# Expert layers of a fused attention and mixture-of-experts kernel: the last float64 conversion step of each expert moved into its first layer, two softmax operations rewritten, and row transposes on full blocks

## The chip, the cores and the metric

The kernel runs on one core of one Trainium2 chip. The time is the device time of one execution in microseconds (us), first instruction to last with what lies around them. A core has TensorE for matrix products (PE in the rows, with PEld for the loading of its stationary operand), VectorE (DVE), ScalarE (ACT), GpSimd (POOL) and SyncE (SP), whose queue here only issues transfers. All of them run their own instructions in order and wait for one another through semaphores.

## The reference

Three parts follow each other: a recurrent attention over 768 steps, a mixture of 8 experts in which each of the 3072 rows goes to the expert with the largest logit, and a dense layer of width 2048.

```python
def _moe_ref(x, w_gate, w_output_gate, w1, w2):
    logits = x @ w_gate
    e_idx = np.argmax(logits, axis=1)
    probs = np.exp(logits - logits.max(-1, keepdims=True))
    probs /= probs.sum(-1, keepdims=True) + 1e-09
    gate_w = probs[np.arange(N), e_idx]
    eom = 1.0 / (1.0 + np.exp(-(x @ w_output_gate)))
    for e in range(E):
        mask = e_idx == e
        h = np.maximum(x[mask] @ w1[e], 0.0)
        out[mask] = gate_w[mask, None] * eom[mask, e, None] * (h @ w2[e])

def _moe2_ref(x, w_in, w_out):
    h = np.maximum(x @ w_in, 0.0)
    return (h * h @ w_out).astype(np.float32)
```

The weights w_in and w_out of the dense layer come as float64; all else is float32.

## The kernel before

The attention comes first; while it runs, the rows are sorted by expert in DRAM. Then the experts follow, in the order 0 to 7, written out by hand instruction by instruction (nothing reorders them), and then the dense layer.

**An expert.** Up to 448 rows of an expert stand transposed in `x3`. The *first layer* has eight parts f = 0 to 7: eight matmuls with 448 columns fill `ph` in PSUM (three buffers), and `hidden` empties it: ScalarE writes the rectified high part (L1304), VectorE the low part (L1305). A `ph` buffer is free again when VectorE is done with it, so part f + 3 of TensorE waits for VectorE's part f. At the ends of f = 5, 6 and 7, `trans_x` transposes a third of the next expert's rows each (L1277, four blocks of up to 128 rows; the last block has 64), which `split_x` splits on ScalarE and VectorE. The *second layer* has 64 matmuls (L1408) in eight groups t = 0 to 7; `beside(e, t, gate)` issues the work of other engines at the start of each group. Its three results `py` are copied by ScalarE (L1415, then L1413 twice) and stored. Expert 0 is split: its first 256 rows run through all f ahead of the loop over the experts, the other rows in the loop.

**Weight pieces.** `drain(later, 1)` converts one piece of the next expert's weights: ScalarE rounds it (L920), GpSimd subtracts (L921), and SP then issues the load of a later piece (L958). Four pieces are in f = 0 to 3, four at t = 0, 2, 4 and 6. After the last expert's pieces come those of w_in.

**Conversion steps.** `Narrow` turns w_in and w_out from float64 into float32, in 32 pieces. `narrow.load()` issues the load of a piece (q, L1185). `narrow.step()` number i issues the store of piece i - 2 from ScalarE's queue (L1206), converts piece i (ScalarE L1193, VectorE L1194 to L1197, GpSimd L1198), and finishes piece i - 1 on VectorE (L1211). 34 steps are needed. One stands at the end of expert 0's first 256 rows, four in each second layer at t = 1, 3, 5 and 7, and one behind the last expert.

**Factors.** `gates` computes the rows' factors for `gt` at t = 1 to 3: maximum and difference on VectorE (L1023, L1024), two exponentials on ScalarE (L1026, L1027), then on VectorE a copy (L1029), a sum (L1031), an addition (L1032), and three more small operations (L1033 to L1035).

**The dense layer** begins with `stage1`: eight matmuls with 512 columns into `ph2` (two buffers), emptied by ScalarE (L1454) and squared and split by VectorE and ScalarE (L1455 to L1457). `stage2` (L1229 to L1231) multiplies by w_out.

Of the kernel before, what the change touches and what calls it, by code (L numbers as in the profile page):

```python
# [12 lines left out]
AF = mybir.ActivationFunctionType  # L13
ALU = mybir.AluOpType
# [10 lines left out]
E = 8  # L25
# [798 lines left out]
def program(tc, A, out, nch=NCH, order=ORDER):  # L824
    nc = tc.nc
    V, G, S_, P = nc.vector, nc.gpsimd, nc.scalar, nc.tensor
    with ExitStack() as top:
# [113 lines left out]
        def drain(g, n=10**6):  # L941
            for _ in range(n):
                if next(g, "end") == "end":
                    return
# [71 lines left out]
        def gates(pool, x, g, e):  # L1016


            a8 = list(x.shape[:-1]) + [8]
            L, O = x[..., 0:8], x[..., 8 + e]  # L1020
            d = pool.tile(a8, F32, name="gd", bufs=1)
            m = pool.tile(a8[:-1], F32, name="gm", bufs=1)
            V.tensor_reduce(out=m, in_=L, axis=AX.X, op=ALU.max)  # L1023
            V.tensor_tensor(out=d, in0=L, in1=m.unsqueeze(len(a8) - 1).to_broadcast(a8), op=ALU.subtract)  # L1024
            yield
            S_.activation(d, d, AF.Exp)  # L1026
            S_.activation(g[..., 1], O, AF.Exp, scale=-1.0)  # L1027
            yield
            V.tensor_copy(g[..., 0], x[..., 16])  # L1029
            g = g[..., 1]  # L1030
            V.tensor_reduce(out=m, in_=d, axis=AX.X, op=ALU.add)  # L1031
            V.tensor_scalar(out=m, in0=m, scalar1=1e-9, scalar2=None, op0=ALU.add)  # L1032
            V.scalar_tensor_tensor(out=g, in0=g, scalar=1.0, in1=m, op0=ALU.add, op1=ALU.mult)  # L1033
            V.reciprocal(g, g)
            V.tensor_tensor(out=g, in0=g, in1=g, op=ALU.mult)  # L1035

# [235 lines left out]

        def transpose(t, pk, ks, js):
            for j in js:
                n = NBLK[j]
                for k in ks:
                    P.transpose(pk[k][:, 128 * j : 128 * j + n], t[0:n, j, 128 * k : 128 * k + 128], ident[0:n, 0:n])  # L1277

        with ExitStack() as ctx:
            ep = ctx.enter_context(tc.tile_pool(name="ep", bufs=1))  # L1280
# [32 lines left out]
            with tc.manual_schedule():  # L1313
                S_.activation(fl[:, 0:1], cst[0:1, 0:1], AF.Exp)
                load_x(0)
                trans_x(0, range(3), raws[:, 3].rearrange("p (j x)->p j x", j=2), range(2))
                py = psy.tile([128, 320], F32, name="py", tag="py")
                for _ in range(4):
                    P.matmul(py[:, 0:128], ident, ident, start=True, stop=True)
                drain(first_w[0])  # L1320
                cur = parts(ring[0], 6144)
                narrow = Narrow()
                later = stream([(e % 2, A["we"][e], W1E) for e in range(1, E)] + [(0, wiD, W2I)], before)
                drain(later, 1)
                load_x(1)
                h = [ep.tile([128, 2 * CAP], F32R, name="hw", bufs=9) for f in range(8)]
                for f in range(8):
                    ph = psh.tile([128, CAP], F32, name="ph")
                    first(ph[:, 0:256], *cur, F1, f, x3[0], slice(0, 256))
                    hidden(ph, h[f], slice(0, 256))  # L1330
                    if f == 5:
                        trans_x(0, range(3), None, range(2, 4))
                    if f in (4, 7):
                        drain(later, 1)
                    if f < 4:
                        narrow.load()
                    if f == 7:
                        narrow.step()

                def put(j, n, off, gt):  # L1340
                    why = "the experts have at most S * B rows together"
                    p = min(n, 128)
                    at = nc.s_assert_within(off + 128 * j, 0, YR - n, skip_runtime_bounds_check_because=why)
                    nc.sync.dma_start(out=gtD[bass.ds(at, n)].rearrange("(j p) x->p j x", p=p), in_=gt[0:p, j : j + n // p])

                def factors(e, off):

                    gt = mp.tile([128, 4, 2], F32, name="gt", bufs=2)
                    yield from gates(mp, glog.pop(e), gt, e)
                    yield  # L1350
                    put(0, 384, off, gt)
                    rest.append((3, 64, off, gt))

                def beside(e, t, gate):

                    if t == 0 and e + 2 < E:
                        load_x(e + 2)
                    if t % 2 == 0:
                        drain(later, 1)
                    else:  # L1360
                        narrow.step()
                    if t == 2:
                        narrow.load()
                    if t > 0:
                        drain(gate, 1)

                glog, rest = {}, []
                for e in range(E):
                    hi, lo = parts(ring[e % 2], 6144)
                    gl = glog[e] = mp.tile([128, 4, 18], F32, name="gl", bufs=2)  # L1370
                    S_.activation(gl, xg[e][:, :, 384:XW], AF.Copy)
                    if e == E - 1:
                        load_y(E)
                    off = nc.values_load(oi[0:1, e : e + 1], engines=[mybir.EngineType.SP], min_val=0, max_val=Y0 + S * B)
                    if e:
                        h = [ep.tile([128, 2 * CAP], F32R, name="hw", bufs=9) for f in range(8)]
                    for f in range(8):
                        ph = psh.tile([128, CAP], F32, name="ph")
                        c = slice(0 if e else 192, CAP)
                        first(ph[:, c], hi, lo, F1, f, x3[e], c)  # L1380
                        hidden(ph, h[f], slice(0 if e else 256, CAP))
                        if f in (range(4) if e else (1, 3)):
                            drain(later, 1)
                        if e and 4 <= f < 7:
                            narrow.load()
                        if f == 7 and rest:
                            put(*rest.pop())
                        if f >= 5:
                            if e + 1 < E:
                                trans_x(e + 1, [f - 5])  # L1390
                            else:
                                split_y(E, f - 5)
                    gate = factors(e, off)
                    why = "the experts have at most S * B rows together"
                    col = nc.s_assert_within(off, 0, YR - CAP, skip_runtime_bounds_check_because=why)
                    wc = ring[e % 2][:, 5120:6144].bitcast(F32R)

                    seq = [(2, f, k) for f in range(8) for k in range(2)] + [(m, f, k) for m in range(2) for f in range(8) for k in range(3)]
                    for i, (m, f, k) in enumerate(seq):
                        if i % 8 == 0:  # L1400
                            beside(e, i // 8, gate)
                        last = f == 7 and k == 2 - (m == 2)
                        if f == 0 and k == 0:
                            py = psy.tile([128, CAP], F32, name="py", tag="py")
                        x = h[f][:, CAP * (k == 1) : CAP * (k == 1) + CAP]
                        c = 3072 + 256 * f + 128 * m
                        w = (hi, hi, lo)[k][:, c : c + 128] if m < 2 else wc[:, 128 * f : 128 * f + 128]
                        P.matmul(py, w, x, start=(f == 0 and k == 0), stop=last)  # L1408
                        if last:
                            yT = xp.tile([128, CAP], F32, name="yT", bufs=3)  # L1410
                            n = 128 if m < 2 else 64
                            if m < 2:
                                S_.activation(yT, py, AF.Copy)  # L1413
                            else:
                                S_.activation(yT[0:64], py[64:128], AF.Copy)  # L1415
                                V.tensor_tensor(out=yT[0:64], in0=py[0:64], in1=yT[0:64], op=ALU.add)
                            nc.sync.dma_start(out=yTD[128 * m : 128 * m + n, bass.ds(col, CAP)], in_=yT[0:n])
                    drain(gate)
                narrow.step()
                assert narrow.at >= len(narrow.todo) + 2  # L1420


# [106 lines left out]
```

## Time and profile before

| | |
|---|---|
| median of 3 runs | 1053.68 us (1048.99 to 1054.67) |
| the profiled execution | 1044.5 us, of which the span from first to last instruction is 1042.7 us |
| attention | 0 to 442 us |
| experts | 442 to 681 us |
| dense layer | 681 to 1042.7 us |
| mean granted TensorE clock | 0.971 of full speed |

The profiled execution was 9.2 us shorter than the median of the runs. Times of a part are read from the trace, in us from the span's start. Durations of single instructions are in us, or in ns where a row says mean ns.

### The profile page before, as it was taken

How to read it: one execution, taken by the hardware profiler on the slowest of the kernel's cores; microseconds unless marked ns; L12 is line 12 of the kernel's file. 1: busy time of each engine (PE TensorE's matmuls, PEld its weight loads, DVE VectorE, ACT ScalarE, POOL GpSimd, SP SyncE). 2: the span in 40 equal slices, each digit the busy share in tenths (PEclk: the TensorE clock that was granted, in tenths of full speed). 3: DMA queues.
4: the chain of work that ended last, by engine and by line, in shares of the span. 5: the costliest groups of instructions: out<-in, count | busy, mean ns of one | idle time of the engine just before them, and what ended most of it. 6: DMA issues, size and time to landing. Idle time of an engine off the chain costs nothing.

```text
span 1042.7 us, 33206 instructions
## 1 busy us (share of the span) xinstructions
PE 945.3 (91%) x13882; PEld 832.5 (80%) x13882; DVE 689.9 (66%) x1768; ACT 606.8 (58%) x1350; POOL 464.0 (45%) x449
## 2 busy tenths in 40 slices
PE   1679988989898988799999999989999999999997
PEld 1567777877777776688888889979988899988986
DVE  5889999899888985447777777665444343434341
ACT  3568987978888888345554455544433343433332
POOL 5657777676777764337655666620010101010101
PEclk9789999999999998889999999999999999999999
DMA  3864444444434426286898787763101010000000
GB/s 107 262 183 127 126 133 120 116 114 107 127 105 128 123 58 171 65 268 162 227 240 229 231 224 191 228 121 73 42 13 31 26 31 26 1 26 1 14 13 26
DMA packets 59314, 120.33 MB, mean 115 GB/s; under 512 B 14608, under 2 KB 32144, under 8 KB 57232
## 3 DMA queue, kind: packets, MB, share of 16 engines
q1 hardware_dynamic: 51424, 103.09, 35.8%
q10 hardware_dynamic: 5040, 6.12, 2.6%
q0 software_dynamic: 2688, 8.88, 2.5%
q8 instruction: 112, 1.84, 0.8%
q14 instruction: 50, 0.41, 0.1%
HBM read 92.01 MB, written 26.05 MB: 113 GB/s over the span
## 4 chain that ended last, share of the span: by engine, by line
PE 66%; DVE 16%; ACT 7%; DMA 6%; issue 4%; SPq 1%; POOL 1%; POOLq 0%; ACTq 0%; DVEq 0%
PE ph L1226 24%; PE po L1230 5%; PE po L1229 5%; PE po L1231 5%; PE py L1408 4%; PE ST L659 3%; PE tp L696 2%; DMA q<-in_wi_dram 2%; ACT sT L676 2%; PE sc L715 2%; PE kt L543 2%; PE y L732 2%; PE R L629 2%; DVE c L1194 2%; PE lg L872 1%
## 5 line engine op out<-in xcount | busy, mean ns | idle before, releaser
L1226 PE MATMUL ph<-x,ring 128*128 128x512 f32 (+2 forms) x1344 | 311.8, 380 | 9.6 <-DVE hw L1305 5.8
L1226 PEld LDWEIGHTS ph<-x,ring 128*128 128x128 f32 x1344 | 241.7, 191 | 46.4 <-DVE hw L1305 8.1
L1480 POOL DMA_INDIRECT out_dram<-o,TID x24 | 27.8, 1158 | 322.7 <-ACT o L1478 281.4
L921 POOL TENSOR_TENSOR ring<-raws,ring 128x732 fp32r<-128x732 f32 (+2 forms) x72 | 123.7, 1734 | 59.4 <-DVE x L1220 28.0
L1455 DVE TENSOR_TENSOR q<-r 128x512 f32<-128x512 f32 x96 | 66.5, 692 | 121.9 <-ACT r L1454 121.9
L1454 ACT ACTIVATE r<-ph 128x512 f32<-128x512 f32 x96 | 57.3, 597 | 126.6 <-PE ph L1226 124.3
L486 POOL TENSOR_TENSOR arena<-arena 40x1024 f32<-40x1024 f32 x43 | 105.6, 2455 | 36.4 <-DVE arena L468 12.1
L1229 PE MATMUL po<-ring,hh 128*128 128x320 f32 x368 | 114.2, 310 | 0.0
L1230 PE MATMUL po<-ring,hl 128*128 128x320 f32 x368 | 114.1, 310 | 0.0
L1231 PE MATMUL po<-ring,hh 128*128 128x320 f32 x368 | 113.8, 309 | 0.0
L1457 DVE TENSOR_TENSOR hl<-q,hh 128x512 fp32r<-128x512 f32 x92 | 63.8, 693 | 64.2 <-ACT hh L1456 64.2
L1408 PE MATMUL py<-hw,ring 128*128 128x448 f32 x512 | 105.8, 367 | 0.0
L1408 PEld LDWEIGHTS py<-hw,ring 128*128 128x128 f32 x512 | 95.6, 188 | 7.9
L1456 ACT ACTIVATE hh<-q 128x512 fp32r<-128x512 f32 x92 | 58.1, 632 | 70.1 <-DVE q L1455 70.1
L1229 PEld LDWEIGHTS po<-ring,hh 128*128 128x128 f32 x368 | 69.6, 189 | 4.3
L1230 PEld LDWEIGHTS po<-ring,hl 128*128 128x128 f32 x368 | 69.4, 189 | 3.9
L1305 DVE SCALAR_TENSOR_TENSOR hw<-ph,hw 128x448 fp32r<-128x448 f32 (+2 forms) x72 | 40.0, 570 | 49.1 <-ACT hw L1304 49.0
L1231 PEld LDWEIGHTS po<-ring,hh 128*128 128x128 f32 x368 | 69.3, 188 | 0.0
L1304 ACT ACTIVATE hw<-ph 128x448 fp32r<-128x448 f32 (+2 forms) x72 | 36.0, 501 | 42.2 <-PE ph L1226 42.1
L1198 POOL TENSOR_TENSOR c<-c,r 128x384 int32<-128x384 int32 (+1 forms) x32 | 35.1, 1097 | 52.0 <-issue 15.6
L920 ACT ACTIVATE ring<-raws 128x732 fp32r<-128x732 f32 (+2 forms) x72 | 57.0, 794 | 1.5 <-DMA raws<-in_we_dram 1.1
L676 ACT ACTIVATE sT<-ST 40x320 f32<-40x320 f32 x88 | 33.1, 424 | 34.7 <-PE ST L659 34.5
(214 smaller groups left out, 1974.1 us busy)
## 6 DMA issues: line engine op xcount, KB each, us to landing
raws<-in_we_dram SPq DMA_DIRECT2D x48, 366.0 KB
arena<-in_xE_dram SPq DMA_DIRECT2D x48, 322.5 KB
xL<-in_xL_dram SPq DMA_DIRECT2D x24, 480.0 KB
xsD<-raws SPq DMA_DIRECT2D x24, 268.0 KB
q<-in_wi_dram SPq DMA_DIRECT2D x16, 384.0 KB
xg<-xsD SPq DMA_DIRECT2D x7, 804.0 KB
q<-in_wo_dram SPq DMA_DIRECT2D x16, 320.0 KB
wb<-in_wB_dram SPq DMA_DIRECT2D x24, 165.0 KB
```

The costliest lines, as they stand in the source:

```text
L486: (V if c < EARLY[2 + hh] else G).tensor_tensor(out=bd[sl, :, :, hh].rearrange("p a b c l j->p (a b) c (l j)"), in0=s["bk"][sl].rearrange( ...
L920: S_.activation(hi, rw, AF.Copy)
L921: G.tensor_tensor(out=lo, in0=rw, in1=hi.bitcast(F32), op=ALU.subtract)
L1226: P.matmul(ps, t[:, o : o + 128], x3[:, i, c], start=(j == 0), stop=(j == 7))
L1229: P.matmul(ps, hh, whi[:, o : o + 320], start=start, stop=False)
L1230: P.matmul(ps, hl, whi[:, o : o + 320], start=False, stop=False)
L1231: P.matmul(ps, hh, wlo[:, o : o + 320], start=False, stop=stop)
L1408: P.matmul(py, w, x, start=(f == 0 and k == 0), stop=last)
L1454: S_.activation(r, ph, AF.Relu)
L1455: V.tensor_tensor(out=q, in0=r, in1=r, op=ALU.mult)
L1456: S_.activation(hh, q, AF.Copy)
L1457: V.tensor_tensor(out=hl, in0=q, in1=hh.bitcast(F32), op=ALU.subtract)
```

## The change

Three edits stand side by side.

1. The steps of `Narrow` at t = 7 are gone, and so are the one at the end of expert 0's first 256 rows and the one behind the last expert. In their place, each expert has a step in the middle of its first layer, behind `hidden` of f = 4. Expert 7 has two more, at t = 6 and t = 7, which only finish and store the last pieces. There are still 34 steps in the same order.
2. In `gates`, the copy into `g[..., 0]` and the addition of 1 run on ScalarE, and the addition of 1e-9 is joined to the multiplication: four VectorE operations become two, and ScalarE gets two.
3. `transpose` takes 128 rows for the last block as well. Its rows 64 to 127 are computed and not used.

```diff
-            V.tensor_copy(g[..., 0], x[..., 16])
+            S_.activation(g[..., 0], x[..., 16], AF.Copy)
             g = g[..., 1]
+            S_.activation(g, g, AF.Copy, bias=1.0)
             V.tensor_reduce(out=m, in_=d, axis=AX.X, op=ALU.add)
-            V.tensor_scalar(out=m, in0=m, scalar1=1e-9, scalar2=None, op0=ALU.add)
-            V.scalar_tensor_tensor(out=g, in0=g, scalar=1.0, in1=m, op0=ALU.add, op1=ALU.mult)
+            V.scalar_tensor_tensor(out=g, in0=m, scalar=1e-9, in1=g, op0=ALU.add, op1=ALU.mult)
...
             for j in js:
-                n = NBLK[j]
                 for k in ks:
-                    P.transpose(pk[k][:, 128 * j : 128 * j + n], t[0:n, j, 128 * k : 128 * k + 128], ident[0:n, 0:n])
+                    P.transpose(pk[k][:, 128 * j : 128 * j + 128], t[:, j, 128 * k : 128 * k + 128], ident)
...
                     if f < 4:
                         narrow.load()
-                    if f == 7:
-                        narrow.step()
...
                     if t % 2 == 0:
                         drain(later, 1)
-                    else:
+                    elif t < 7:
                         narrow.step()
                     if t == 2:
                         narrow.load()
+                    if e == E - 1 and t >= 6:
+                        narrow.step()
...
                         if f in (range(4) if e else (1, 3)):
                             drain(later, 1)
+                        if f == 4:
+                            narrow.step()
                         if e and 4 <= f < 7:
                             narrow.load()
...
                     drain(gate)
-                narrow.step()
```

First VectorE, from t = 5 of expert 3's second layer into expert 4's first layer, in the program before. Here `c_13074`, `c_13035` and `c_13104` are pieces that the steps work on, and `hw` is the hidden layer.

```order
L1194 TENSOR_SCALAR c_13074<-q_12949 128x384
L1195 TENSOR_SCALAR c_13074<-c_13074 128x384
L1196 TENSOR_SCALAR c_13074<-c_13074 128x384
L1197 TENSOR_SCALAR c_13074<-c_13074 128x384
L1211 SCALAR_TENSOR_TENSOR c_13035<-q_12928,c_13035 128x384
L1194 TENSOR_SCALAR c_13104<-q_13021 128x384
L1195 TENSOR_SCALAR c_13104<-c_13104 128x384
L1196 TENSOR_SCALAR c_13104<-c_13104 128x384
L1197 TENSOR_SCALAR c_13104<-c_13104 128x384
L1211 SCALAR_TENSOR_TENSOR c_13074<-q_12949,c_13074 128x384
L1305 SCALAR_TENSOR_TENSOR hw<-ph,hw 128x448 x6
L1217 TENSOR_TENSOR x_13226<-pk,x_13226 128x448
```

The same place now; the piece that was `c_13104` is named `c_13202`, and `hidden` is at L1304.

```order
L1197 TENSOR_SCALAR c_13074<-c_13074 128x384
L1211 SCALAR_TENSOR_TENSOR c_13035<-q_12928,c_13035 128x384
L1304 SCALAR_TENSOR_TENSOR hw<-ph,hw 128x448 x5
L1194 TENSOR_SCALAR c_13202<-q_13021 128x384
L1195 TENSOR_SCALAR c_13202<-c_13202 128x384
L1196 TENSOR_SCALAR c_13202<-c_13202 128x384
L1197 TENSOR_SCALAR c_13202<-c_13202 128x384
L1211 SCALAR_TENSOR_TENSOR c_13074<-q_12949,c_13074 128x384
L1304 SCALAR_TENSOR_TENSOR hw<-ph,hw 128x448
L1217 TENSOR_TENSOR x_13226<-pk,x_13226 128x448
```

The five operations of the last step stood ahead of all six hidden parts, and now stand between the fifth and the sixth.

Then ScalarE at the end of the last expert, in the program before, from t = 5 on; `c_14534` is the last piece, and L1454 is the first operation of the dense layer.

```order
L1206 DMA woD<-c_14456 128x320
L1193 ACTIVATE r_14535<-q_14426 128x320
L920 ACTIVATE ring_9072<-raws 128x768
L1206 DMA woD<-c_14496 128x320
L1413 ACTIVATE yT<-py 128x448
L1206 DMA woD<-c_14534 128x320
L1454 ACTIVATE r_14605<-ph_14596 128x512
```

The same place now, with the copy of the result at L1414.

```order
L1206 DMA woD<-c_14456 128x320
L1193 ACTIVATE r_14535<-q_14426 128x320
L920 ACTIVATE ring_9072<-raws 128x768
L1206 DMA woD<-c_14496 128x320
L1206 DMA woD<-c_14534 128x320
L1414 ACTIVATE yT<-py 128x448
L1454 ACTIVATE r_14605<-ph_14596 128x512
```

The store of the last piece has moved ahead of the copy of the last result; both stand ahead of the dense layer's first operation, as before.

Last TensorE, in expert 1's first layer, as one piece of the difference; `pk` is the PSUM tile of the transposes.

```order
 L1226 MATMUL ph<-x_12342,ring_12071 128x448 x48
-L1277 MATMUL pk<-cst,xg 128x128 x3
-L1277 MATMUL pk<-cst,xg 128x64
+L1276 MATMUL pk<-cst,xg 128x128 x4
 L1226 MATMUL ph<-x_12342,ring_12071 128x448 x8
```

The fourth transpose of each group of four now has the shape of the other three.

## Rows read from the trace of the kernel before

**Rows 1.** Experts: busy time (count) of PE, PEld, DVE, ACT, POOL; granted clock, DMA share, GB/s.

```profile
442.00:681.00 239.00, 232.58 (x1192) 209.82 (x1193) 169.84 (x326) 124.39 (x246) 140.12 (x94) 0.99 0.78 221
```

**Rows 2.** TensorE's waits from 442 to 694 us: total, times, longest.

```profile
PE ph L1226 <- DVE hw L1305: 5.8, 5, 2.1
```

**Rows 3.** TensorE and ScalarE, timeline: start, length, idle before; experts 0 and 4, dense layer.

```profile
452.26 5.01 PE L1226 MATMUL ph<-x,ring 128*128 128x256 f32 x40
457.41 0.54 ACT L1193 ACTIVATE r<-q 128x384 int32<-128x384 uint32 x1 [1.85 <-DMA q<-in_wi_dram]
459.37 4.63 PE L1226 MATMUL ph<-x,ring 128*128 128x256 f32 x24 [2.10 <-DVE hw L1305]
...
574.97 5.07 PE L1226 MATMUL ph<-x,ring 128*128 128x448 f32 x24 [0.81 <-DVE hw L1305]
...
688.69 3.57 PE L1226 MATMUL ph<-x,ring 128*128 128x512 f32 x8 [3.77 <-ACT r L1454]
```

**Rows 4.** Busy time and granted clock, as in rows 1, behind two stalls.

```profile
461.00:464.00 3.00, 3.00 (x17) 3.00 (x17) 0.71 (x2) 1.14 (x3) 2.64 (x2) 0.55 0.41 95
688.69:692.05 3.36, 3.36 (x8) 2.62 (x9) 2.67 (x4) 1.74 (x3) 0.00 (x0) 0.54 0.89 328
```

**Rows 5.** VectorE, timeline at the start of expert 4.

```profile
570.24 0.55 DVE L1211 SCALAR_TENSOR_TENSOR c<-q,c 128x384 int32<-128x384 int32 x1
570.71 1.15 DVE L1194 TENSOR_SCALAR c<-q 128x320 int32<-128x320 int32 x1
...
574.29 1.68 DVE L1305 SCALAR_TENSOR_TENSOR hw<-ph,hw 128x448 fp32r<-128x448 f32 x3
```

**Rows 6.** Transposes: weight loads as a group (idle before), then timelines, experts 0 and 4.

```profile
L1277 PEld LDWEIGHTS pk<-cst,xg 64*128 64x128 f32 x24 | 3.1, 137 | 3.7 <-issue 3.7
...
451.41 0.35 PEld L1277 LDWEIGHTS pk<-cst,xg 128*128 128x128 f32 x3
451.93 0.26 PEld L1277 LDWEIGHTS pk<-cst,xg 64*128 64x128 f32 x3 [0.17 <-issue]
...
579.88 0.69 PE L1277 MATMUL pk<-cst,xg 128*128 128x128 f32 x4
580.50 1.87 PE L1226 MATMUL ph<-x,ring 128*128 128x448 f32 x8
582.21 0.69 PE L1277 MATMUL pk<-cst,xg 128*128 128x128 f32 x4
```

**Rows 7.** Expert 6, first layer: TensorE, GpSimd, VectorE, timeline.

```profile
626.71 9.79 PE L1226 MATMUL ph<-x,ring 128*128 128x448 f32 x48
636.34 0.69 PE L1277 MATMUL pk<-cst,xg 128*128 128x128 f32 x4
...
631.54 6.96 POOL L921 TENSOR_TENSOR ring<-raws,ring 128x732 fp32r<-128x732 f32 x4
...
635.52 0.62 DVE L1305 SCALAR_TENSOR_TENSOR hw<-ph,hw 128x448 fp32r<-128x448 f32 x1 [0.98 <-ACT hw L1304]
...
641.81 0.63 DVE L1305 SCALAR_TENSOR_TENSOR hw<-ph,hw 128x448 fp32r<-128x448 f32 x1 [1.21 <-ACT hw L1304]
```

**Rows 8.** End of expert 7, timelines of VectorE, ScalarE and GpSimd.

```profile
673.79 0.33 DVE L1194 TENSOR_SCALAR c<-q 128x320 int32<-128x320 int32 x1 [3.58 <-DMA q<-in_wo_dram]
...
680.72 1.68 DVE L1032 TENSOR_SCALAR gm<-gm 128x4 f32<-128x4 f32 x1
...
685.56 2.08 DVE L1211 SCALAR_TENSOR_TENSOR c<-q,c 128x320 int32<-128x320 int32 x1 [0.75 <-POOL c L1198]
...
685.22 0.54 ACT L1413 ACTIVATE yT<-py 128x448 f32<-128x448 f32 x1 [3.71 <-PE ph L1226]
...
688.04 0.60 ACT L1454 ACTIVATE r<-ph 128x512 f32<-128x512 f32 x1 [2.28 <-DVE c L1211]
...
685.49 1.79 POOL L921 TENSOR_TENSOR ring<-raws,ring 128x768 fp32r<-128x768 f32 x1
```

**Rows 9.** A small operation of ScalarE in the factors, as a group: busy us, mean ns.

```profile
L1027 ACT ACTIVATE gt<-gl 128x4 f32<-128x4 f32 x8 | 1.5, 193 | 0.0
```

## The prediction

> **What bounds the kernel now.** I read the busy times by stretch first. Among the experts TensorE is busy for 232.58 of 239 us [rows 1]; VectorE, ScalarE and GpSimd are not. So time comes only out of two things: TensorE's gaps, and what TensorE itself does. For the gaps I read its waits: five of them, 5.8 us together, are for VectorE's low half of a hidden part, the longest 2.1 us [rows 2]. The timeline places them. One is in expert 0, the other four (5.8 - 2.1 = 3.7 us) stand three parts behind the start of experts 1 to 4, as the 0.81 us of expert 4, and a sixth, 3.77 us for ScalarE, is in the dense layer's third part [rows 3]. After the two long ones the granted clock is 0.55 and 0.54, about the lower of its two levels, 1.2 GHz [rows 4].
>
> Who is late? At expert 4 TensorE starts the first layer at 569.18 us (574.97 less the gap and three parts of 1.6). VectorE is then still in the steps of t = 5 and t = 7: the last one holds it from 570.71 until the hidden parts start at 574.29, three at a stretch [rows 5]. TensorE's fourth part starts at 574.97, when the first of the three is done.
>
> **Edit 1, the steps.** *Expert 0.* ScalarE waits for the first piece until 457.41 us, ahead of the hidden parts, and TensorE loses 2.10 us. Its next 24 matmuls take 4.63 us; at the rate just before (40 in 5.01) it would be 3.0, so the clock takes 1.6 more [rows 3, 4]. The step now comes five parts later, when the piece has landed. Term: 3.7; at worst, half.
>
> *Experts 1 to 4.* Without the step at t = 7, VectorE is free 3.6 us earlier (574.29 - 570.71 [rows 5]), while the gaps are near 0.9. Term: 3.7; at worst nothing, if VectorE is late for another reason.
>
> *What the step costs in its new place.* Its queue entries are the same: a store from ScalarE's queue, one operation of ScalarE, five of VectorE, one of GpSimd. On VectorE, four operations of 0.33 [rows 8] and one of 0.55 [rows 5] make about 2.0 us. Take expert 6, with T = 626.71. VectorE ends part 4 at 636.14 (T + 9.4) and begins part 7 at 641.81 [rows 7]: 5.7 us, in which it has two hidden parts of 0.62 and two splits of the same size, so 3.2 us are idle. The second layer starts near T + 14.9 (636.34, two periods of 2.33 and 0.62 [rows 6, 7]); part 7 ends 0.8 us behind that, and its low half is needed at the 16th matmul, 3.0 us behind. So the step may hold VectorE for 3.2 + 2.2 = 5.4 us before TensorE waits. The PSUM buffers do not tighten this: part 7 needs the buffer of part 4, which is emptied ahead of the step. GpSimd's four splits end at T + 11.8 today [rows 7], so a step that began at T + 9.4 could meet them for 2.4 us; 4.4 is still under 5.4, and they should end earlier, since t = 7's operation no longer stands ahead of them. On SP, the third load of a piece (f = 6) now waits for this step, as it reuses the buffer that the step frees; behind it stand the factors' store and the next weights and rows, all used many us later. Term: 0.
>
> *The dense layer.* ScalarE begins it at 688.04, behind the store of the last piece, which waits for VectorE's L1211; that ran from 685.56 for 2.08 us, up to the end of GpSimd's split at 687.28 and its own time [rows 8]. The two steps at t = 6 and 7 leave these operations in their order. What shortens the chain is the missing addition (L1032, 1.68 us on 4 columns), and an earlier start: the chain begins with a wait of 3.58 us for a loaded piece [rows 8], whose issue stands on SP behind GpSimd's four splits. At most the gap goes, with the slow clock behind it: eight matmuls took 3.36 us [rows 4], eight at 448 columns take 1.6 [rows 7], so 1.83 at 512, and 1.5 are lost: 3.77 + 1.5 = 5.3. At least nothing: L1032's wait may pass to the next operation, and the copy of 0.54 us [rows 8] now follows the store. I take 3.5, nearer the upper end, because the gap needs only to fall well below expert 0's 2.1 us for the clock to stay.
>
> **Edit 2, the factors.** ScalarE gains 16 operations; the nearest row has 0.19 us [rows 9], so 3.1 us in all, or 0.4 an expert. They lie at t = 3, where ScalarE waits for TensorE's results; it is busy for 124 of 239 us [rows 1]. Without that cover they would cost 3.1. VectorE's gain is already in the terms above and is not counted again.
>
> **Edit 3, the transposes.** The 24 weight loads with 64 rows stand behind 3.7 us of idle time that waits for nothing, 0.17 each at 22 places (in expert 0 three follow each other) [rows 6]. From one group of four transposes to the next TensorE takes 582.21 - 579.88 = 2.33 us [rows 6]. At 48 matmuls in 9.63 us (636.34 - 626.71 [rows 7]) the eight matmuls are 1.605, so four transposes cost 0.725. Loads with 128 rows follow each other in (0.35 - 0.14) / 2 = 0.105 us [rows 6]; four such are 0.42, which saves 0.30 at each of 21 places: 6.3 us. On the other side: loads with 64 rows follow each other in (0.26 - 0.14) / 2 = 0.06, so if the gap stayed, 24 wider ones would cost 24 x 0.045 = 1.1 us. I take 6.3, since the gap stands before the 64-row load and at no other in the run of four.
>
> By the Trainium skill, "TensorE: Matmul & The Clock Gate", section "Back-to-back issue gap", a matmul's gap grows with its columns, about 60 cycles up to 64 and 134 at 128; an estimate from that page is 24 x 74 / 2.4 GHz = 0.7 us lost and nothing gained. The rows speak against it here, as the narrow one is the slow one.
>
> **Sum.** 3.7 + 3.7 + 3.5 + 6.3 = 17.2 us. The profiled execution took 1044.5 us (a span of 1042.7 and 1.8 around it) and would take 1027.3. The runs' median, 1053.68, lay 9.2 higher; the terms are TensorE's own gaps, so I take them off the median: **1036.5 us**.
>
> **Rivals.**
> *The end of expert 7 stays as it is* (the addition's wait passes to the next VectorE operation, and the copy behind the store eats the rest). For it: GpSimd's splits run on there, and 2.08 us for one L1211 shows it [rows 8]. The term of 3.5 goes: 1040.0. Chance 0.15.
> *The transposes don't pay*: the idle time belongs to the last transpose of a group and not to its 64 rows. Against it: expert 0, where the gap stands ahead of the first of three [rows 6]. 6.3 turns into -1.1: 1043.9. Chance 0.10.
> *The moved step doesn't free VectorE*: DMA engines are busy to 0.78 [rows 1], pieces land later, and the steps of t = 1 to 5 still end late. Experts 1 to 4 and the dense layer give nothing: 1043.7. Chance 0.07.
> *Slower:* each of the step's four VectorE operations waits for one of GpSimd's splits, 6.96 / 4 = 1.74 us [rows 7]. Then the step takes 7.0 + 2.0 = 9.0 us, 3.6 over the room of 5.4, and eight experts lose 29 us: 1065. It decides from 5.4 us a step, and eats all gains at 5.4 + 17.2 / 8 = 7.6. For it: L1194 took 1.15 instead of 0.33 at the splits' side [rows 5, 8]. Against: the splits would have to run 7 us beyond T + 9.4, where today 2.4 remain [rows 7]. Chance 0.06. The Trainium skill, "SBUF — State Buffer", section "SBUF: two separate sides", says that VectorE and GpSimd take a shared pair of ports as a lock for a whole instruction, the other blocked meanwhile. By that rule each of the four could wait for a whole split; the durations above agree with it.
>
> **How the numbers follow.** The forecast has 0.62. The range goes down to 1027 (the profiled execution less the sum) and up to 1048: the first two rivals together leave 17.2 - 7.4 - 3.5 = 6.3, or 1047.4. 0.5% is 5.3 us, about what a measurement of this kernel can tell from no change. Faster by more: the forecast, the first rival, and most of the next two, which leave 9.8 and 10.0, 0.89. The same: a part of these and of the last, 0.06. Slower: 0.05.
>
> **What would show it.** Edit 1: no wait of TensorE for L1304 at the start of experts 1 to 4, and none at 459 us; clock 1.00 there. A VectorE step behind part 4 of about 2 to 4 us, with no wait in the second layer's first 16 matmuls. Edit 3: 2.03 us from one group of transposes to the next, and no idle time before their weight loads. The dense layer: a gap under 1 us at its third part. I am wrong if TensorE waits in the second layer, if the dense layer's gap stays near 3.8, or if the period stays at 2.33.

## The result, and the profile after

The changed kernel takes 1040.93 us (median of 11 runs, 1035.07 to 1047.17), the one before 1054.67 (11 runs, 1046.56 to 1059.75). The ratio is 0.9882, with a 95% interval of 0.9847 to 0.9917: the median is 13.7 us less, where 17.2 were forecast. The interval of the ratio is 8.8 to 16.1 us.

The profiled execution took 1040.41 us (span 1038.6). It is compared by stretch, because the two profiled executions differ in the attention, whose instructions the change leaves alone. The experts run here from the first `ph` matmul to the first one with 512 columns, the dense layer from there to the end of the span.

| us | attention | experts | dense layer | span |
|---|---|---|---|---|
| before | 445.0 | 236.0 | 361.7 | 1042.7 |
| after | 454.5 | 221.3 | 362.7 | 1038.6 |
| difference | +9.5 | -14.7 | +1.0 | -4.1 |

So the spans show 4.1 and the medians 13.7. The two stretches that the change touches give the same sum (-14.7 + 1.0), which is closer than the interval of the ratio can tell. Over all ten profiles of this study the attention took between 438.9 and 455.4 us.

The first view of after is TensorE's waits, as in [rows 2]: total, times, longest.

```profile
PE ph L1226 <- ACT r L1454: 4.5, 1, 4.5
...
```

The five waits for VectorE are gone. One wait for ScalarE is left, and it is longer than the 3.77 us of [rows 3]. The busy times by stretch, as in [rows 1] and [rows 4], show the experts and then what follows that wait:

```profile
454.50:675.87 221.37, 221.37 (x1180) 205.07 (x1180) 159.25 (x306) 124.10 (x256) 139.07 (x93) 1.00 0.79 235
...
684.30:687.50 3.20, 3.19 (x9) 2.52 (x10) 2.50 (x4) 1.74 (x3) 0.00 (x0) 0.61 0.99 371
```

Among the experts TensorE is busy for all of 221.37 us at a granted clock of 1.00. Behind the gap in the dense layer the clock is 0.61, lowered as in [rows 4] (0.54).

Where the moved step stands, VectorE's timeline in expert 5:

```profile
603.74 0.63 DVE L1304 SCALAR_TENSOR_TENSOR hw<-ph,hw 128x448 fp32r<-128x448 f32 x1 [1.02 <-ACT hw L1303]
604.28 0.85 DVE L1194 TENSOR_SCALAR c<-q 128x320 int32<-128x320 int32 x1
605.16 0.33 DVE L1195 TENSOR_SCALAR c<-c 128x320 f32<-128x320 f32 x1
...
606.13 0.48 DVE L1211 SCALAR_TENSOR_TENSOR c<-q,c 128x320 int32<-128x320 int32 x1
606.53 0.62 DVE L1304 SCALAR_TENSOR_TENSOR hw<-ph,hw 128x448 fp32r<-128x448 f32 x1
```

The step takes 606.6 - 604.28 = 2.3 us. Its first operation, L1194, takes 0.85 where it takes 0.33 elsewhere [rows 8], so it is held for half a microsecond; the others run at their own length, and the next hidden parts follow without a wait of TensorE. In the other experts L1194 takes 0.81 to 1.52 at this place, and TensorE does not wait there either.

The transposes of expert 4, on TensorE, as in [rows 6]:

```profile
577.40 0.60 PE L1276 MATMUL pk<-cst,xg 128*128 128x128 f32 x4
577.75 1.85 PE L1226 MATMUL ph<-x,ring 128*128 128x448 f32 x8
579.45 0.60 PE L1276 MATMUL pk<-cst,xg 128*128 128x128 f32 x4
```

From one group to the next it is 579.45 - 577.40 = 2.05 us, where it was 2.33.

Last the start of the dense layer, the engines mixed in order of time, as in [rows 8]:

```profile
669.67 0.33 DVE L1194 TENSOR_SCALAR c<-q 128x320 int32<-128x320 int32 x1 [3.40 <-DMA q<-in_wo_dram]
...
675.92 0.55 DVE L1033 SCALAR_TENSOR_TENSOR gt<-gm,gt 128x4 f32<-128x4 f32 x1
...
676.41 1.86 POOL L921 TENSOR_TENSOR ring<-raws,ring 128x768 fp32r<-128x768 f32 x1
...
676.72 1.56 DVE L1035 TENSOR_TENSOR gt<-gt 128x4 f32<-128x4 f32 x1
...
680.68 1.79 POOL L921 TENSOR_TENSOR ring<-raws,ring 128x768 fp32r<-128x768 f32 x1
680.75 2.08 DVE L1211 SCALAR_TENSOR_TENSOR c<-q,c 128x320 int32<-128x320 int32 x1 [0.75 <-POOL c L1198]
...
683.23 0.54 ACT L1414 ACTIVATE yT<-py 128x448 f32<-128x448 f32 x1 [5.82 <-DVE c L1211]
683.67 0.59 ACT L1454 ACTIVATE r<-ph 128x512 f32<-128x512 f32 x1
...
684.31 3.24 PE L1226 MATMUL ph<-x,ring 128*128 128x512 f32 x8 [4.53 <-ACT r L1454]
```

Read it upwards. TensorE's third part waits for ScalarE's L1454. That stands behind the copy L1414, which ScalarE reached 5.82 us late, because the store ahead of it waited for VectorE's L1211. L1211 needed 2.08 us: GpSimd's split of 680.68 ended at 682.47, and L1211 ended its own time of about 0.4 us behind that. Higher up, L1035, on 4 columns, now takes 1.56 us beside another split.

### The profile page after: what moved, and what is told of

Read it like the earlier page. It is cut to its first block, busy times and chain, and to the rows that moved or that the text cites. A ratio compares the mean times of both kernels' runs of the same rounds, so it can differ in the third digit from the quotient of the medians.

```text
span 1038.6 us, 33215 instructions
## 1 busy us (share of the span) xinstructions
PE 944.7 (91%) x13882; PEld 835.9 (80%) x13882; DVE 683.0 (66%) x1752; ACT 610.8 (59%) x1366; POOL 463.6 (45%) x449
## 4 chain that ended last, share of the span: by engine, by line
PE 51%; DMA 2%; DVE 1%; issue 1%; ACT 0%; POOLq 0%; POOL 0%; ACTq 0%; DVEq 0%; SPq 0%
PE ph L1226 26%; PE py L1409 9%; PE po L1230 5%; PE po L1229 5%; PE po L1231 5%; PE pk L1276 1%; DMA out_dram<-o,TID 1%; DMA q<-in_wo_dram 1%; DMA yTD<-yT 1%; DMA xg<-yTD 0%; DVE c L1211 0%; DVE c L1194 0%; PE py L1318 0%; POOLq L1524 0%; ACT r L1454 0%
## 5 line engine op out<-in xcount | busy, mean ns | idle before, releaser
L1226 PE MATMUL ph<-x,ring 128*128 128x512 f32 (+2 forms) x1344 | 308.1, 378 | 4.5 <-ACT r L1454 4.5
L1455 DVE TENSOR_TENSOR q<-r 128x512 f32<-128x512 f32 x96 | 66.4, 691 | 122.5 <-ACT r L1454 122.5
L1454 ACT ACTIVATE r<-ph 128x512 f32<-128x512 f32 x96 | 57.3, 597 | 124.4 <-PE ph L1226 124.4
L1457 DVE TENSOR_TENSOR hl<-q,hh 128x512 fp32r<-128x512 f32 x92 | 63.8, 693 | 64.1 <-ACT hh L1456 64.1
L1409 PEld LDWEIGHTS py<-hw,ring 128*128 128x128 f32 x512 | 95.5, 188 | 7.9
L1456 ACT ACTIVATE hh<-q 128x512 fp32r<-128x512 f32 x92 | 58.1, 632 | 70.1 <-DVE q L1455 70.1
L1304 DVE SCALAR_TENSOR_TENSOR hw<-ph,hw 128x448 fp32r<-128x448 f32 (+2 forms) x72 | 41.0, 570 | 51.6 <-ACT hw L1303 51.6
L920 ACT ACTIVATE ring<-raws 128x732 fp32r<-128x732 f32 (+2 forms) x72 | 56.8, 790 | 4.8 <-DMA raws<-in_we_dram 4.2
L1198 POOL TENSOR_TENSOR c<-c,r 128x384 int32<-128x384 int32 (+1 forms) x32 | 35.1, 1098 | 49.5 <-ACT yT L1414 12.0
```

Source lines behind the costliest of these rows:

```text
L920: S_.activation(hi, rw, AF.Copy)
L1226: P.matmul(ps, t[:, o : o + 128], x3[:, i, c], start=(j == 0), stop=(j == 7))
L1454: S_.activation(r, ph, AF.Relu)
L1455: V.tensor_tensor(out=q, in0=r, in1=r, op=ALU.mult)
L1456: S_.activation(hh, q, AF.Copy)
L1457: V.tensor_tensor(out=hl, in0=q, in1=hh.bitcast(F32), op=ALU.subtract)
```

## The experiments

Two things were to be told apart: which edit gave the 14.7 us among the experts, and why the dense layer gave none. The theory on the second: the chain of steps t = 6 and t = 7 stands ahead of L1414 and L1454 in ScalarE's queue and ends in a GpSimd split, whatever happens to the factors. The rival was that a shorter chain of factors does shorten it.

**Each edit alone.** Three kernels apply edit 1 (steps_only), edit 2 (factors_only) or edit 3 (transposes_only) of the diff above to the kernel before, and nothing else.

> The kernel before with edit 1 alone. Theory: the moved steps remove the gaps at expert 0 (2.1 us and 1.6 of slow clock) and at experts 1 to 4 (3.7), so the stretch from the first expert matmul to the first dense one falls from 236.0 us to about 228.6, and the dense layer's gap is 3.8 to 4.6, the copy of 0.54 now being behind the store. Rival: the gaps went because of the two VectorE operations that edit 2 takes away; then gaps of 0.4 us or more stay at experts 1 to 4 and the stretch is 231 or more.

> The kernel before with edit 2 alone. Theory: most of what the two removed operations took was a wait for GpSimd, which passes on to the next VectorE operations; VectorE ends the second layer's work 0.5 to 1 us earlier, the gaps at experts 1 to 4 shrink by that (2 to 3 us together), expert 0 keeps its 2.1, the dense layer's gap stays between 3 and 4. Expert stretch 233 to 235 us. Rival: the whole 2.5 us per expert come off VectorE's chain: no gaps at experts 1 to 4, a dense gap near 1.3, stretch 232.3.

> The kernel before with edit 3 alone. Theory: TensorE saves 0.28 us at each of 22 places, but VectorE's steps do not come earlier by as much, so the gaps at experts 1 to 4 grow by up to 0.8 each and experts 5 and 6 can get new ones: the expert stretch falls by 2 to 5 us (231 to 234), not by 6.1. Rival: the terms add, TensorE's gaps stay as long as they were, and the stretch is 229.9.

| | experts | dense layer | its gap | ratio to before, 95% interval |
|---|---|---|---|---|
| before | 236.0 | 361.7 | 3.77 | |
| steps only | 227.4 | 363.7 | 4.88 | 0.9943 (0.9898 to 0.9987) |
| factors only | 232.5 | 361.4 | 3.32 | 0.9981 (0.9942 to 1.0021) |
| transposes only | 231.1 | 362.8 | 3.83 | 0.9993 (0.9952 to 1.0034) |
| all three | 221.3 | 362.7 | 4.53 | 0.9882 (0.9847 to 0.9917) |

The whole times of the three can hardly be told from one another (only that of the steps lies clear of 1), but the stretches can, each from one profile. Three profiles with the same instructions among the experts (the changed kernel, and late_end and split_behind below) agree there within 0.3 us. The steps give 8.6 us among the experts and lengthen the dense gap, here to just over the expected 4.6. The transposes give 4.9; the gaps of experts 1 to 4 stay, at 0.92 to 1.25. The factors give 3.5, which was closer to the rival's figure: freeing VectorE at t = 3 removes most of the same gaps at experts 1 to 4 (0.43 and 0.25 are left at two of them), and the dense gap keeps 3.32. The three sum to 17.0 and together give 14.7, since factors and steps buy the same gaps.

**The end of the last expert.** First (late_end), the two last steps go behind the dense layer's third and fourth part:

```diff
-                    if e == E - 1 and t >= 6:
-                        narrow.step()
...
                     if n % 2 == 0:
                         drain(wout, 1)
+                    if n in (2, 3):
+                        narrow.step()
```

> The changed kernel with the last two steps (which finish and store the last pieces) behind the dense layer's third and fourth part instead of at t = 6 and 7 of expert 7. Theory: the dense gap of 4.5 us is ScalarE standing at the store of the last piece, which waits for VectorE's L1211, which waits for GpSimd; without that order ScalarE copies and begins the dense layer as soon as TensorE is done. Gap under 1 us, no slow clock behind it, dense stretch 362.7 less 5 to 6 us, ratio to before near 0.983. Rival: VectorE is as late with its steps of t = 5, so the first dense squares come late all the same and the gap only moves one part on: dense stretch less 0 to 2 us.

The dense layer takes 357.6 us, 5.1 less than in the changed kernel. The experts stay at 221.6. Its timeline (L1451 is here what L1454 was, L1454 what L1457 was):

```profile
655.17 0.33 DVE L1194 TENSOR_SCALAR c<-q 128x320 int32<-128x320 int32 x1 [2.61 <-DMA q<-in_wo_dram]
...
662.20 1.56 DVE L1035 TENSOR_TENSOR gt<-gt 128x4 f32<-128x4 f32 x1
662.47 5.79 PE L1226 MATMUL ph<-x,ring 128*128 128x512 f32 x24
...
664.54 0.60 ACT L1451 ACTIVATE r<-ph 128x512 f32<-128x512 f32 x1 [1.23 <-PE ph L1226]
...
665.40 1.36 DVE L1452 TENSOR_TENSOR q<-r 128x512 f32<-128x512 f32 x1
...
669.08 0.41 PE L1230 MATMUL po<-ring,hl 128*128 128x320 f32 x1 [0.56 <-DVE hl L1454]
...
669.81 0.42 PE L1231 MATMUL po<-ring,hh 128*128 128x320 f32 x1 [0.33 <-DVE ring L1250]
```

Three parts run without a gap, though L1035 waits for its split as before. ScalarE now waits for TensorE, not the reverse. The kernel takes 1028.72 us (6 runs); its ratio to before is 0.9790 (0.9714 to 0.9866). It beats the kernel before. That it also beats the changed kernel rests on the stretch: the two intervals overlap a little (that of the changed kernel is 0.9847 to 0.9917), and the attention of its profile, 440.9 us, was a short one. The 5.1 us hold against the one profile of the changed kernel. Against narrow_first below, which has the same end of expert 7 as the changed kernel and a dense layer of 360.5 us, it is 2.9.

Second (split_behind), the weight piece of t = 6 goes behind the last step, so that no split runs beside L1211:

```diff
-                    if t % 2 == 0:
+                    if t % 2 == 0 and not (e == E - 1 and t == 6):
                         drain(later, 1)
-                    elif t < 7:
+                    elif t % 2 and t < 7:
                         narrow.step()
...
+                    if e == E - 1 and t == 7:
+                        drain(later, 1)
```

> The changed kernel, with GpSimd's last weight split of expert 7 (t = 6) issued behind the two last steps instead of ahead of them. Theory: VectorE's last L1211 takes 2.08 us in place of 0.49 because that split starts at the same moment and holds GpSimd's side for its 1.8; with the split behind it, L1211 takes about 0.5 and the dense gap falls from 4.5 to about 2.9 us. Rival: L1211 is long for a reason of its own (what it reads was just written), and stays near 2.1; the gap stays at 4.5.

```profile
664.27 0.49 DVE L1211 SCALAR_TENSOR_TENSOR c<-q,c 128x320 int32<-128x320 int32 x1 [0.76 <-POOL c L1198]
...
666.09 1.82 POOL L921 TENSOR_TENSOR ring<-raws,ring 128x768 fp32r<-128x768 f32 x1 [1.85 <-ACT ring L920]
...
666.96 1.50 DVE L1457 TENSOR_TENSOR q<-r 128x512 f32<-128x512 f32 x1 [2.20 <-ACT r L1456]
666.98 2.14 PE L1226 MATMUL ph<-x,ring 128*128 128x512 f32 x8 [2.81 <-ACT r L1456]
```

L1211 takes 0.49 us in place of 2.08. So the length of L1211 was the split's. The gap falls to 2.81, close to what was expected, but only about half of that fall comes from L1211. From the landing of the piece (L1194 at 653.17) to L1456 it is 13.17 us, where the changed kernel has 14.00 from 669.67 to 683.67. That is 0.8 less and not 1.6, because the rounding of the moved piece (L920, 0.84 us) now stands on ScalarE ahead of the copy and L1456. The rest is that the piece landed 0.9 us earlier, counted from the first matmul of expert 7 (19.18 against 20.07 us), with the same instructions up to there. The split then holds the squaring of the dense layer (L1457 here, L1455 in the changed kernel), 1.50 in place of 0.69, and two further gaps of 0.68 and 0.30 follow. The dense layer takes 360.8, 1.9 less than in the changed kernel and about as much as in narrow_first (360.5), which leaves L1211 as it is; so no gain of this order is shown. This is one run (1022.89 us, with an attention of 438.9).

Third (late_end_no_factors), late_end with the old factors (edit 2 undone):

> The late end again, with the factors as in the kernel before (edit 2 undone). Theory: with no step at t = 7 VectorE has time to spare at the end of each second layer, so edit 2 is worth nothing beside edit 1: expert stretch 221 to 222.5 us and dense stretch 357 to 358.5, as in the late end with it. Rival: it is worth what it is worth alone, 3.5 us, and gaps stand again at experts 1 to 4: stretch near 225.

```profile
668.30 5.79 PE L1226 MATMUL ph<-x,ring 128*128 128x512 f32 x24
...
668.54 1.69 DVE L1032 TENSOR_SCALAR gm<-gm 128x4 f32<-128x4 f32 x1
...
672.55 1.36 DVE L1452 TENSOR_TENSOR q<-r 128x512 f32<-128x512 f32 x1
...
675.26 0.41 PE L1229 MATMUL po<-ring,hh 128*128 128x320 f32 x1 [1.18 <-ACT ring L1249]
```

The experts take 221.7 us, 0.1 more than with edit 2. So edit 2 gives nothing there once the steps are moved. But the dense layer takes 360.7 against 357.6, which the expectation missed. VectorE's first squaring (L1452) starts 672.55 - 668.30 = 4.25 us behind the first dense matmul, against 665.40 - 662.47 = 2.93 in late_end. About half of these 1.3 us is the old factors' longer chain (from the landed piece to the squaring it is 0.7 us longer), the other half is that the piece landed 0.6 us later in this profile. How much of the 3.1 us is edit 2's is therefore not shown. Three gaps, 2.04 us together, replace two of 0.89, and the clock falls:

```profile
677.00:681.00 4.00, 4.00 (x15) 3.79 (x16) 2.61 (x5) 2.38 (x4) 0.00 (x0) 0.57 0.87 303
```

The kernel takes 1032.25 us (4 runs), ratio 0.9845 (0.9777 to 0.9914), which can't be told from late_end's.

**The slower rival, put in its place (step_at_f1).** The step goes behind f = 1, into the middle of GpSimd's splits:

```diff
-                        if f == 4:
+                        if f == 1:
                             narrow.step()
```

> The changed kernel with each expert's first step behind f = 1 of the first layer instead of f = 4, where GpSimd's four splits are still to come. Theory (the slower rival of the prediction put in its place): each of the step's four VectorE operations waits for a split under way, the step holds VectorE for 5 to 8 us, the hidden part f = 2 is late for TensorE's f = 5, and seven experts lose 1 to 4 us each: expert stretch 228 to 249 us. Rival: VectorE gets in between the splits at small cost, the step takes under 3 us as at f = 4, no gaps, stretch near 221.5.

```profile
PE ph L1226 <- DVE hw L1304: 4.8, 8, 1.4
...
564.04 4.88 POOL L921 TENSOR_TENSOR ring<-raws,ring 128x512 fp32r<-128x512 f32 x3
...
566.72 0.57 DVE L1194 TENSOR_SCALAR c<-q 128x320 int32<-128x320 int32 x1
...
567.33 1.78 DVE L1195 TENSOR_SCALAR c<-c 128x320 f32<-128x320 f32 x1
...
569.96 1.06 POOL L1198 TENSOR_TENSOR c<-c,r 128x320 int32<-128x320 int32 x1 [1.04 <-ACT hw L1303]
...
570.98 3.49 POOL L921 TENSOR_TENSOR ring<-raws,ring 128x732 fp32r<-128x732 f32 x2
```

The first row is one of TensorE's waits, the others the timeline in expert 4. All eight experts get a gap, 4.8 us together, TensorE's first-layer matmuls are busy for 2.6 us more, and the experts take 228.7 us, 7.4 more. The step takes 570.30 - 566.72 = 3.6 us: one of its operations, L1195, waits for a whole split, not four, and so it is in all eight experts. The splits behind that stand on GpSimd behind the step's own L1198, so VectorE can only meet those issued ahead of the step. The stretch is at the near end of what was expected, but a step of 3.6 us is not the 5 to 8 that were expected to cause it. It is one run, 1036.69 us.

**The transposes, narrow one first (narrow_first).** The 64-row transpose of before comes back, but as the first of its four:

```diff
-            for j in js:
+            for j in sorted(js, key=lambda j: NBLK[j]):
+                n = NBLK[j]
                 for k in ks:
-                    P.transpose(pk[k][:, 128 * j : 128 * j + 128], t[:, j, 128 * k : 128 * k + 128], ident)
+                    P.transpose(pk[k][:, 128 * j : 128 * j + n], t[0:n, j, 128 * k : 128 * k + 128], ident[0:n, 0:n])
```

> The changed kernel with the 64-row transposes of the kernel before, but as the first of each group of four and not the last. Theory: a switch between 64 and 128 rows costs about 0.1 to 0.17 us on either side of the narrow one, wherever it stands: the idle time stays with the 64-row weight load or its successor, and the period from group to group is 2.30 to 2.35 us, expert stretch near 227. Rival: the idle time belongs to the last transpose of a group; then it stands ahead of a 128-row load at the end of the group, or is gone, with a period near 2.05.

```profile
575.76 0.52 PEld L1277 LDWEIGHTS pk<-cst,xg 64*128 64x128 f32 x4 [0.30 <-issue]
576.24 1.53 PEld L1226 LDWEIGHTS ph<-x,ring 128*128 128x128 f32 x8
578.07 0.51 PEld L1277 LDWEIGHTS pk<-cst,xg 64*128 64x128 f32 x4 [0.30 <-issue]
```

The idle time moves with the 64-row load to the head of the group. The period is 578.07 - 575.76 = 2.31 us, as before the change (2.33), and the experts take 227.0, 5.7 more than with 128 rows throughout. So the cost belongs to the narrow transpose and not to the last place. Whether it is its rows or its columns that cost was not tried. One run, 1039.17 us.

## Why the prediction was right, and where not

**Expert 0** was forecast at 3.7 us. The groups of TensorE among the experts (busy us, mean ns, idle before) are for before

```profile
L1226 PE MATMUL ph<-x,ring 128*128 128x448 f32 x448 | 96.8, 370 | 3.7 <-DVE hw L1305 3.7
L1226 PE MATMUL ph<-x,ring 128*128 128x256 f32 x128 | 18.7, 309 | 2.1 <-DVE hw L1305 2.1
```

and for after

```profile
L1226 PE MATMUL ph<-x,ring 128*128 128x448 f32 x448 | 95.5, 368 | 0.0
L1226 PE MATMUL ph<-x,ring 128*128 128x256 f32 x128 | 16.8, 291 | 0.0
```

The 256-column matmuls are expert 0's own: 18.7 + 2.1 - 16.8 = 4.0. Right.

**Experts 1 to 4**, forecast at 3.7: the idle time went, and with it 96.8 - 95.5 = 1.3 us of busy time, together 5.0. The mechanism was right and the term too small. A gap of before cost more than the wait that the row gives it: steps_only, which keeps the transposes of before, has the 95.5 too. (The prediction's start of expert 4, 569.18 us, is the trace's; its working gives 569.36, and nothing hangs on it.)

**The transposes**, forecast at 6.3: 21 x (2.33 - 2.05) = 5.9. Right, and narrow_first shows that the narrow transpose was its cause. By the Trainium skill, "TensorE: Matmul & The Clock Gate", section "Back-to-back issue gap", the wider ones would have lost an estimated 0.7. The trace shows a gain of 5.9 in its place. The page's figures go by columns alone and the narrow transpose has fewer rows as well, so whether its rule on columns fails here is not shown.

**The step in its new place**, forecast at 0: right, 2.3 us of VectorE and no wait. step_at_f1 shows that the slower rival is a real mechanism, but its price, a split for each of four operations, was too high. One operation waited for a split. The Trainium skill, "SBUF — State Buffer", section "SBUF: two separate sides", describes a lock held for a whole instruction, which a VectorE operation takes in a two-port mode or with two inputs from SBUF. The 1.78 us of L1195 agree with such a lock. How many operations met a split was set here by the order of GpSimd's own queue.

**The dense layer** was forecast at 3.5 and gave -1.0; its gap grew from 3.77 to 4.53, which the prediction had named as a sign that it is wrong there. This is the step that failed: "What shortens the chain is the missing addition (L1032, 1.68 us on 4 columns), and an earlier start". The table takes the gap apart. Times are in us from the first matmul of expert 7 (654.58 before, 649.60 after); "piece lands" is the start of L1194 behind its wait for the loaded piece, and "first operation" is ScalarE's first one of the dense layer (L1454 before and after).

| | piece lands | first operation | between | gap |
|---|---|---|---|---|
| before | 19.21 | 33.46 | 14.25 | 3.77 |
| transposes only | 19.49 | 33.73 | 14.24 | 3.83 |
| factors only | 19.30 | 32.86 | 13.56 | 3.32 |
| steps only | 19.74 | 34.42 | 14.68 | 4.88 |
| all three | 20.07 | 34.07 | 14.00 | 4.53 |
| narrow_first | 18.32 | 32.35 | 14.03 | 2.80 |

Edit 2, with the missing addition, shortens the chain by 0.7 us, with the moved steps (14.68 to 14.00) and without them (14.25 to 13.56), and not by 1.68. Most of the addition's wait passed on, as the first rival said. Before:

```profile
679.74 0.86 DVE L1029 COPY gt<-gl 128x4 f32<-128x4 f32 x1
...
682.50 0.17 DVE L1033 SCALAR_TENSOR_TENSOR gt<-gt,gm 128x4 f32<-128x4 f32 x1
...
682.92 0.16 DVE L1035 TENSOR_TENSOR gt<-gt 128x4 f32<-128x4 f32 x1
```

L1029 and L1032, 0.86 + 1.68 us, are gone, but L1033 and L1035 now take 0.55 and 1.56. Edit 1 lengthens the chain by 0.4, as the copy of 0.54 us now follows the store. Together the edits take 0.25 off it.

The start was not earlier but 0.86 later, and TensorE got to its third part 0.15 sooner: 0.86 - 0.25 + 0.15 = 0.76, by which the gap grew. That the change delayed the piece is not shown. Up to there late_end and split_behind have the same instructions as the changed kernel, and in them it landed at 18.98 and 19.18. In narrow_first, whose end of expert 7 is that of the changed kernel, it landed at 18.32:

```profile
668.92 0.33 DVE L1194 TENSOR_SCALAR c<-q 128x320 int32<-128x320 int32 x1 [2.40 <-DMA q<-in_wo_dram]
...
680.02 2.09 DVE L1211 SCALAR_TENSOR_TENSOR c<-q,c 128x320 int32<-128x320 int32 x1 [0.77 <-POOL c L1198]
...
683.59 3.51 PE L1226 MATMUL ph<-x,ring 128*128 128x512 f32 x8 [2.80 <-ACT r L1455]
```

The chain is as long as in the changed kernel, and the gap smaller by as much as the piece was earlier. Why it lands at different times is open. So the sign of the -1.0 is the profile's (the dense layer takes 362.7 us in the changed kernel, 361.9 in step_at_f1 and 360.5 in narrow_first), but 3.5 us come out in none of them.

The first rival's time was 1040.0, and the measured one is 1040.93. Of the bound for this term, up to 5.3, late_end takes 5.1 against the changed kernel's profile and 2.9 against narrow_first's, by moving the steps out of the chain.

**The factors** cost nothing on ScalarE, as forecast. What the prediction did not say is that they buy the gaps of experts 1 to 4 a second time (3.5 us alone, 0.1 with the steps moved).

**The sum** is then 4.0 + 5.0 + 5.9 = 14.9 for the three terms among the experts, against 14.7 by the stretch, and -1.0 for the dense layer. The dense term missed by 4.5 us and the whole by 3.5 (17.2 against 13.7): it was in part luck that the term of experts 1 to 4 was 1.3 too small. Taking the terms off the median and not off the profiled execution fits the two profiles: with the attention of after, 9.5 us longer, the profiled execution of before would have taken 1054.0, near the median of 1054.67.

## What to carry to other kernels

Before counting an operation's long duration as a gain, ask what it waited for: if it waited for another engine's work, most of the wait can pass to the next operation that needs the same thing (here 0.7 of 1.68 us were saved), and moving one of the two out of the chain can pay more. Before putting a gap's change down to an edit, take the gap apart into where its chain starts and how long the chain is: here the start alone moved by up to 1.1 us with the same instructions. An instruction that no one waits for yet, such as the store of a converted piece, still delays what stands behind it in its engine's queue. Where two edits both free the same engine ahead of the same gap, their gains don't add.

## What the runs showed of the hardware

The attention took from 438.9 to 455.4 us with the same instructions, also on one chip (440.9 to 455.4 in four kernels). Where this spread comes from is open; a difference of a few us between two spans says nothing here without the stretches.

The clock fell behind gaps that are short one by one: the 1.18, 0.53 and 0.33 us of late_end_no_factors were followed by 0.57, while in step_at_f1 a single gap of 1.41 us at expert 0 was not: the eight matmuls behind it take 1.22 us, the next eight 1.19. With 0.56 and 0.33 in late_end it stayed at 1.00. The length of a gap alone does not decide: behind the 2.81 us of split_behind the eight matmuls with 512 columns take 2.14 us at 1.00, behind the 2.80 of narrow_first they take 3.51, with the clock at 0.50. Behind the gaps of 1.86 and 1.85 at expert 0 in factors_only and transposes_only it fell to 0.52 and 0.50. The prediction took a gap well below 2.1 us as enough for the clock to stay; these rows give no such limit.

L1035, on 128x4 elements, takes 0.16 to 0.17 us in the kernel before and 1.46 to 1.56 in the changed one, where it stands beside a split of GpSimd; L1032 took 1.58 to 1.68 there before. That is almost as long as operations on 80 times the columns (L1195, 1.78 on 320).
